# Reordering the first batch of a retention and wave-MLP kernel around its fourth pair

## The chip, the cores and the metric

The kernel runs on one core of a Trainium2 chip. The metric is the time of one execution on the device in microseconds (us). TensorE is called PE here, its weight loads PEld, VectorE DVE, ScalarE ACT, GpSimd POOL and SyncE SP, as in the profile.

## What is computed

There are B = 4 batches, H = 8 heads, S = 768 steps and head size D = 64. First comes a retention recurrence, then a token and channel mixer on its output x of shape (4, 768, 512):

```
state = gamma[h] * state + outer(k[t], v[t])
x[t]  = scale * (q[t] @ state)                  # per batch and head

theta = x @ w_theta
zr, zi = x * cos(theta), x * sin(theta)
y = w_tok_r @ zr + w_tok_i @ zi                 # over the tokens of a batch
u = x + y
out = u + max(u @ w_ch, 0)
```

All inputs and the output are float32. The kernel multiplies in bfloat16.

## The kernel before

**Pairs.** The 768 steps of a batch are cut into three pairs of 2 x 128 steps, so that there are twelve pairs n = 0 to 11, of which 0, 1 and 2 are the first batch. Even and odd steps of a pair are kept apart ("two" in the code). For each pair, `load` brings q, k and v (512 KB each) with one DMA each into a ring of seven buffers. `prep` (L162) casts k to bfloat16 (one instruction on ACT, L169, or elsewhere, L171) and multiplies q and v with the powers of gamma (two halves each, L175, each on a chosen engine: `DP` is DVE and POOL, `PP` twice POOL). `flip` (L179) turns k or q with eight PE transposes into PSUM and copies them out on DVE (L186); later pairs use a DMA transpose instead (`flip_dma`, from pair 7 for k, pair 10 for q).

**Retention.** `ret_A` multiplies turned k and q, `ret_mask` (L211, DVE) applies the causal mask, `ret_Y` adds mask times v, `ret_I` (L241) adds the part of the state, `ret_S` (L258) adds to the state in PSUM, `state_out` (L272, ACT) copies it out, and `ret_out` (L281) copies a half of the result to `xT`. 

**Mixer.** `theta` multiplies xT with w_theta, and ACT makes cosine and sine of it (`cs`, L305 and L306). `x_pe` turns xT back to x (L295, copy L296 on DVE); later pairs do that by DMA. `zmul` (L312, DVE) makes z. `moe_M` (L328) multiplies one row tile of the token weights with all six z tiles of a batch, step s0 by step s0, two matmuls each. `moe_u` (L335, DVE) adds x, `moe_U` turns u (copy L349 on ACT), `moe_O` (L356) multiplies with w_ch, `moe_out` (L363, DVE) finishes, `store` writes a tile. The token weights come as rows: `w_cast` casts a row tile of both parts on POOL (L375) into a ring of three row buffers, `w_tok` turns it with twelve PE transposes (L382) and copies it out, one part on DVE, one on ACT (L386, L388).

**PSUM.** A ring of two buffers, tag "tr", serves all transposes and also `moe_O`. A ring of two, "acc", serves theta and the two halves of `ret_Y`. One bank "at" serves `ret_A`, one bank "st" the state, one bank "y" the sum of `moe_M` until late in the kernel. An instruction that writes a buffer waits until the last reader of its former content is done.

**Order.** There is no scheduler. Each engine runs its instructions in the order in which the Python code issues them. For the first three pairs this order is written out by hand (L450 to L555), and the loop over n at L565 issues the rest: in round n it does the retention of pair n, the theta and z of pair n - 1, the mixer's tiles of the batch before, and the preparation of later pairs. `keep_busy` (L445) issues matmuls on zeros whose result is not used. SP's queue of loads is written out at L111 for the first six pairs and the weights: p0, w_theta, p1, w0, p2, w1, w2, p3, w3, w_ch, p4, w4, p5, w5. Round n issues the loads of pair n + 3.

The round n = 3 (nG is 3) in before prepares pair 4 early: `prep` of q and v on POOL as its first step, `flip` of k and q in its middle, ahead of `ret_S(3, 0)`.

Of the kernel before, what the change touches and what calls it, by code (L numbers as in the profile page):

```python
# [14 lines left out]
FT = mybir.dt.float32  # L15
# [17 lines left out]
def kernel(  # L33
# [142 lines left out]
                                        _bcast_last(sc[:, 2 * g + two], D))  # L176
        st[n, name] = t

    def flip(n, name):  # L179
        ps = psum.tile([P, 2, NP, P], BF, name="kq_ps", tag="tr", bufs=2)  # L180
        for two in range(2):
            for j in range(NP):
                nc.tensor.transpose(ps[:, two, j, :],  # L183
                                    st[n, name][:, two, j * P:(j + 1) * P], ident)
        t = work.tile([P, 2, NP, P], BF, name="kqT", bufs=6)
        nc.vector.tensor_copy(t, ps)  # L186
        st[n, name + "T"] = t

    def flip_dma(n, name):
        t = work.tile([P, 2, NP, P], BF, name="kqT", bufs=6)  # L190
# [18 lines left out]
    def ret_mask(n, two):  # L209
        at, at_ps = work.tile([P, 2, NP, P], BF, name="at", bufs=2), st[n, "at_ps"]  # L210
        nc.vector.tensor_mul(at.rearrange("p a j t -> p (a j) t"),  # L211
                             at_ps.rearrange("p a j t -> p (a j) t"),
                             _bcast_mid(maskp[:, two].rearrange("p w i -> p (w i)"), H))
        st[n, two] = at
# [72 lines left out]
            out=xs[b][:, 2 * g:2 * g + 2, :].rearrange("p a (j e) -> p (a j) e", j=NP),  # L287
            in_=st[n, "xT"].rearrange("p a j t -> p (a j t)"))

    def x_pe(n, lo=0, hi=2):  # L290
        b, g = divmod(n, nG)
        x_ps = psum.tile([P, hi - lo, NP, P], BF, name="x_ps", tag="tr", bufs=2)
        for a in range(lo, hi):
            for j in range(NP):
                nc.tensor.transpose(x_ps[:, a - lo, j, :], st[n, "xT"][:, a, j, :], ident)  # L295
        nc.vector.tensor_copy(xs[b][:, 2 * g + lo:2 * g + hi, :],  # L296
                              x_ps.rearrange("p a j e -> p a (j e)"))

    def theta(n, a):
        th_ps = psum.tile([P, dm], FT, name="th_ps", tag="acc", bufs=2)  # L300
# [16 lines left out]
    def moe_M(m, lo, hi):  # L317
        b, t0 = divmod(m, nT)
        if lo == 0:
            if m < (B - 1) * nT - 1:  # L320
                y_ps = psum.tile([P, dm], FT, name="y_ps", tag="y", bufs=1)
            else:
                y_ps = psum.tile([P, dm], FT, name="y_ps", tag="acc", bufs=2)
            mo[m] = dict(y=y_ps)
        y_ps = mo[m]["y"]
        for s0 in range(lo, hi):
            for r in range(2):
                nc.tensor.matmul(y_ps, wT[r][:, s0, t0 * P:(t0 + 1) * P],  # L328
                                 zs[b][:, s0, r, :], start=(s0 == 0 and r == 0),
                                 stop=(s0 == nT - 1 and r == 1))  # L330
# [40 lines left out]

    def w_cast(t0):
        for r in range(2):
            row = work.tile([P, S], BF, name="wrow", bufs=3)
            nc.gpsimd.tensor_copy(row, wdma[r, t0])  # L375
            wrow[r, t0] = row

    def w_tok(t0):
        for r in range(2):
            w_ps = psum.tile([P, nT, P], BF, name="w_ps", tag="tr", bufs=2)  # L380
            for s0 in range(nT):
                nc.tensor.transpose(w_ps[:, s0, :],  # L382
                                    wrow[r, t0][:, s0 * P:(s0 + 1) * P], ident)
            dst = wT[r][:, :, t0 * P:(t0 + 1) * P]
            if r:
                nc.scalar.copy(dst, w_ps)  # L386
            else:
                nc.vector.tensor_copy(dst, w_ps)  # L388

    def moe_last(m):  # L390

# [53 lines left out]
    def keep_busy(times):  # L445
        for _ in range(times):
            nc.tensor.matmul(warm_ps, warm[:, 0:P], warm, start=True, stop=True)


    DP, PP, K = (nc.vector, nc.gpsimd), (nc.gpsimd, nc.gpsimd), (nc.scalar,)  # L450
    keep_busy(12)
    prep(0, "k", K)
    flip(0, "k")
    keep_busy(4)
    prep(0, "q", DP)
    flip(0, "q")
    keep_busy(2)
    prep(0, "v", PP)
# [3 lines left out]
    keep_busy(2)  # L462
    ret_S(0, 0)
    state_out(0, 0)
    keep_busy(1)
    ret_A(0, 1)
    ret_mask(0, 1)
    ret_S(0, 1)
    state_out(0, 1)
    ret_Y(0, 0)  # L470
    ret_I(0, 1)
    keep_busy(3)
    prep(1, "k", K)
    ret_Y(0, 1)
    ret_out(0, 0, nc.scalar.copy)
    ret_out(0, 1, nc.vector.tensor_copy)
    keep_busy(1)
    flip(1, "k")
    prep(1, "q", DP)
    x_pe(0, 0, 1)  # L480
    theta(0, 0)
    x_pe(0, 1, 2)
    theta(0, 1)
    flip(1, "q")
    keep_busy(2)
    prep(1, "v", PP)
    w_cast(0)
    ret_A(1, 0)
    ret_mask(1, 0)
    keep_busy(2)  # L490
    ret_S(1, 0)
    state_out(1, 0)
    ret_A(1, 1)
    ret_mask(1, 1)
    prep(2, "k", K)
    ret_Y(1, 0)
    ret_I(1, 0)
    ret_S(1, 1)
    state_out(1, 1)
    ret_I(1, 1)  # L500
    keep_busy(2)
    zmul(0, 0)
    zmul(0, 1)
    ret_Y(1, 1)
    ret_out(1, 0, nc.scalar.copy)
    w_tok(0)
    ret_out(1, 1, nc.scalar.copy)
    prep(2, "q", DP)
    flip(2, "k")
    theta(1, 0)  # L510
    flip(2, "q")
    prep(2, "v", PP)
    w_cast(1)
    w_cast(2)
    x_pe(1, 0, 1)
    moe_M(0, 0, 2)
    ret_A(2, 0)
    ret_mask(2, 0)
    theta(1, 1)
    x_pe(1, 1, 2)  # L520
    ret_S(2, 0)
    state_out(2, 0)
    ret_A(2, 1)
    ret_mask(2, 1)
    ret_Y(2, 0)
    ret_I(2, 0)
    ret_I(2, 1)
    zmul(1, 0)
    zmul(1, 1)
    ret_Y(2, 1)  # L530
    ret_out(2, 0, nc.scalar.copy)
    ret_out(2, 1, nc.vector.tensor_copy)
    w_tok(1)
    theta(2, 0)
    x_pe(2, 0, 1)
    theta(2, 1)
    x_pe(2, 1, 2)
    moe_M(0, 2, 4)
    zmul(2, 0)
    prep(3, "k", K)  # L540
    w_tok(2)
    moe_M(0, 4, 5)
    zmul(2, 1)
    flip(3, "k")
    moe_M(0, 5, nT)
    moe_u(0)
    prep(3, "q", DP)
    prep(3, "v", PP)
    w_cast(3)
    moe_M(1, 0, 4)  # L550
    flip(3, "q")
    moe_M(1, 4, nT)
    moe_u(1)
    w_tok(3)
    prep(4, "k", K)  # L555


    tiles_of = {nG - 2: [], nG - 1: [0, 1]}
# [6 lines left out]
    for n in range(nG, B * nG + 1):  # L565
        mine, done = tiles_of[n], tiles_of[n - 1]
        late, two = n > nG, len(mine) > 1
        nxt = n + 1 in pairs

        if nxt and n + 1 >= K_DMA:  # L570
            flip_dma(n + 1, "k")
        if n + 3 in pairs:
            load(n + 3, "k")
        if n >= U_DMA:
            moe_U_dma(done[1])

        if nxt:
            prep(n + 1, "q", PP)
            prep(n + 1, "v", PP)
        if n == nG:  # L580
            w_cast(4)
            nc.gpsimd.tensor_copy(wch, wdma["ch"])
        if n == nG + 1:
            w_cast(5)
        if late:
            ret_I(n - 1, 1)

        if n in pairs:
            ret_A(n, 0)
            ret_mask(n, 0)  # L590
        if late:
            ret_Y(n - 1, 1)
            ret_S(n - 1, 1)
            ret_out(n - 1, 0, nc.scalar.copy)
            ret_out(n - 1, 1, nc.scalar.copy)
            state_out(n - 1, 1)
            if n - 1 >= X_DMA:
                x_dma(n - 1)
        if n + 3 in pairs:
            load(n + 3, "q")  # L600

        first = mine[0]
        moe_M(first, 0, 3 if two else 2)
        if late:
            theta(n - 1, 0)
            if n - 1 < X_DMA:
                x_pe(n - 1)
            theta(n - 1, 1)
        if two:
            moe_M(first, 3, nT)  # L610
            moe_u(first)
        for name, limit in (("k", K_DMA), ("q", Q_DMA)):
            if nxt and n + 1 < limit:
                flip(n + 1, name)
        if not two and n + 1 >= K_DMA:
            moe_M(first, 2, 4)
        if nxt and n + 1 >= Q_DMA:
            flip_dma(n + 1, "q")
        if n + 3 in pairs:
            load(n + 3, "v")  # L620
        for t in tiles_of[n - 2]:
            store(t)
        if n + 1 >= U_DMA:
            moe_U_dma(first)

        if n in pairs:
            ret_S(n, 0)
            state_out(n, 0)
            ret_A(n, 1)
            ret_mask(n, 1)  # L630
            ret_Y(n, 0)
            ret_I(n, 0)
        if n < U_DMA:
            moe_U(done)
        if not two:
            if n + 1 < K_DMA:
                moe_M(first, 2, 4)
            if n in (nG, nG + 1):
                w_tok(n - nG + 4)
            moe_M(first, 4, nT)  # L640
            moe_u(first)
        elif n in pairs:
            moe_M(mine[1], 0, nT)
        if n + 2 in pairs:
            prep(n + 2, "k", K)
        if late:
            zmul(n - 1, 0)
            zmul(n - 1, 1)
        if two and n in pairs:
            moe_u(mine[1])  # L650
        for t in done:
            moe_O(t)
            moe_out(t)
        if n not in pairs:
            moe_M(mine[1], 0, nT)
            moe_u(mine[1])
# [43 lines left out]
```

## Time and profile before

| what | us |
|---|---|
| median of 11 runs | 172.37 |
| lowest and highest | 171.77 to 174.01 |
| the profiled execution | 172.63 |
| span in its profile | 170.9 |
| busy: PE, PEld | 158.5, 89.8 |
| busy: DVE, ACT, POOL | 100.8, 82.6, 62.7 |
| HBM read, written | 25.69 MB, 6.29 MB |

The profile is of one execution. Times in its views run from the start of the span. A busy PE is not yet a PE at its peak, since the matmuls are pipelined: 128 x 512 matmuls are listed with 380 ns each and follow each other every 216 ns. A wait is put down to the instruction that released it last.

### The profile page before, as it was taken

How to read it: one execution, taken by the hardware profiler on the slowest of the kernel's cores; microseconds unless marked ns; L12 is line 12 of the kernel's file. 1: busy time of each engine (PE TensorE's matmuls, PEld its weight loads, DVE VectorE, ACT ScalarE, POOL GpSimd, SP SyncE). 2: the span in 40 equal slices, each digit the busy share in tenths (PEclk: the TensorE clock that was granted, in tenths of full speed). 3: DMA queues.
4: the chain of work that ended last, by engine and by line, in shares of the span. 5: the costliest groups of instructions: out<-in, count | busy, mean ns of one | idle time of the engine just before them, and what ended most of it. 6: DMA issues, size and time to landing. Idle time of an engine off the chain costs nothing.

```text
span 170.9 us, 4674 instructions
## 1 busy us (share of the span) xinstructions
PE 158.5 (93%) x1952; PEld 89.8 (53%) x1979; DVE 100.8 (59%) x139; ACT 82.6 (48%) x141; POOL 62.7 (37%) x81
## 2 busy tenths in 40 slices
PE   7789898979599999999999999999999999999992
PEld 2355565645375766655465655554455544444471
DVE  2357597885457567798477375681755617333443
ACT  8216686770345968767874744828156170000000
POOL 6274839383599678480807254000000000000000
PEclk9999999999969999999999999999999999999999
DMA  4999999999999999989999995986827251554343
GB/s 123 303 342 313 319 316 348 266 377 308 325 287 306 297 294 341 260 192 233 197 282 308 214 278 110 256 101 129 151 44 200 36 168 47 163 157 117 92 153 123
DMA packets 66789, 37.92 MB, mean 222 GB/s; under 512 B 24144, under 2 KB 61264, under 8 KB 66768
## 3 DMA queue, kind: packets, MB, share of 16 engines
q1 hardware_dynamic: 66624, 37.50, 86.8%
q8 instruction: 15, 0.25, 0.6%
q10 hardware_dynamic: 144, 0.13, 0.2%
q14 instruction: 6, 0.05, 0.1%
HBM read 25.69 MB, written 6.29 MB: 187 GB/s over the span
## 4 chain that ended last, share of the span: by engine, by line
PE 79%; DMA 9%; DVE 3%; ACT 3%; issue 2%; POOL 1%; DVEq 0%; POOLq 0%
PE y_ps L328 32%; PE o_ps L356 12%; PE th_ps L302 12%; DMA pair<-in_q_dram 6%; PE at_ps L204 4%; PE kq_ps L183 4%; PE yT_ps L227 4%; PE st_ps L258 3%; PE yT_ps L241 3%; DMA pair<-in_k_dram 2%; PE y_ps L402 2%; PE w_ps L382 2%; DVE at L211 1%; PE u_ps L347 1%; ACT kqb L169 1%
## 5 line engine op out<-in xcount | busy, mean ns | idle before, releaser
L328 PE MATMUL y_ps<-z,wtr 128*128 128x512 bf16 x132 | 50.1, 380 | 1.6 <-DVE u L335 0.9
L328 PE MATMUL y_ps<-z,wti 128*128 128x512 bf16 x123 | 46.7, 380 | 0.5 <-issue 0.2
L175 POOL TENSOR_TENSOR kqb<-pair,qscp 128x512 bf16<-128x512 f32 x20 | 20.6, 1046 | 35.2 <-DMA pair<-in_q_dram 35.2
L335 DVE TENSOR_TENSOR u<-y_ps,x_sb 128x512 bf16<-128x512 f32 x23 | 15.9, 691 | 29.2 <-PE y_ps L328 29.2
L211 DVE TENSOR_TENSOR at<-at_ps,maskp 128x1024 bf16<-128x1024 f32 x24 | 29.2, 1218 | 3.8 <-PE at_ps L204 3.8
L281 ACT CAST xT<-yT_ps 128x512 bf16<-128x512 f32 x22 | 15.0, 738 | 25.7 <-PE yT_ps L227 25.7
L175 POOL TENSOR_TENSOR kqb<-pair,vscp 128x512 bf16<-128x512 f32 x24 | 26.2, 1114 | 2.2 <-DMA pair<-in_v_dram 2.2
L302 PE MATMUL th_ps<-wth,xT 128*128 128x512 bf16 x94 | 23.4, 379 | 0.2
L363 DVE SCALAR_TENSOR_TENSOR ot<-o_ps,u 128x512 f32<-128x512 f32 x23 | 15.8, 689 | 12.4 <-PE o_ps L356 12.4
L356 PE MATMUL o_ps<-wch,uT 128*128 128x512 bf16 x92 | 22.7, 379 | 0.1
L272 ACT CAST stbd<-st_ps 64x256 bf16<-64x256 f32 x40 | 14.7, 368 | 13.2 <-PE st_ps L258 12.5
L328 PEld LDWEIGHTS <-wti 128*128 128x128 bf16 x138 | 13.6, 98 | 14.2 <-issue 1.4
L328 PEld LDWEIGHTS <-wtr 128*128 128x128 bf16 x138 | 13.6, 98 | 14.0 <-issue 0.3
L305 ACT ACTIVATE cs<-th_ps,halfpi 128x512 bf16<-128x512 f32 x24 | 16.5, 689 | 8.3 <-PE th_ps L302 8.0
L186 DVE COPY kqT<-kq_ps 128x1024 bf16<-128x1024 bf16 x17 | 11.5, 687 | 12.4 <-PE kq_ps L183 12.4
L312 DVE TENSOR_TENSOR z<-cs,x_sb 128x1024 bf16<-128x1024 bf16 x24 | 17.1, 748 | 0.7 <-DMA x_sb<-xT 0.7
L306 ACT ACTIVATE cs<-th_ps,zerob 128x512 bf16<-128x512 f32 x24 | 16.5, 688 | 0.0
L356 PEld LDWEIGHTS <-uT 128*128 128x128 bf16 x92 | 8.8, 98 | 10.7 <-ACT uT L349 0.4
L302 PEld LDWEIGHTS <-xT 128*128 128x128 bf16 x96 | 8.9, 98 | 9.9 <-ACT xT L281 0.6
L183 PE MATMUL kq_ps<-ident,kqb 128*128 128x128 bf16 x136 | 10.5, 222 | 3.4 <-POOL kqb L175 1.2
L169 ACT CAST kqb<-pair 128x1024 bf16<-128x1024 f32 x12 | 12.6, 1048 | 1.7 <-DMA pair<-in_k_dram 1.6
L414 ACT COPY uT<-u_ps 128x256 bf16<-128x256 bf16 x2 | 0.7, 372 | 25.6 <-PE u_ps L413 25.6
(57 smaller groups left out, 163.7 us busy)
## 6 DMA issues: line engine op xcount, KB each, us to landing
pair<-in_k_dram SPq DMA_DIRECT2D x12, 512.0 KB, 6.8
pair<-in_q_dram SPq DMA_DIRECT2D x12, 512.0 KB, 7.4
pair<-in_v_dram SPq DMA_DIRECT2D x12, 512.0 KB, 7.7
out_dram<-ot SPq DMA_DIRECT2D x23, 256.0 KB, 2.4
wtok<-in_moe_w_tok_r_dram SPq DMA_DIRECT2D x6, 384.0 KB, 6.9
wtok<-in_moe_w_tok_i_dram SPq DMA_DIRECT2D x6, 384.0 KB, 6.0
w<-in_moe_w_theta_dram SPq DMA_DIRECT2D x1, 1024.0 KB, 8.0
w<-in_moe_w_ch_dram SPq DMA_DIRECT2D x1, 1024.0 KB, 7.2
```

The lines of the kernel that those rows point to most:

```text
L175: engines[two].tensor_mul(dst[:, two], src[:, two], _bcast_last(sc[:, 2 * g + two], D))
L183: nc.tensor.transpose(ps[:, two, j, :], st[n, name][:, two, j * P:(j + 1) * P], ident)
L211: nc.vector.tensor_mul(at.rearrange("p a j t -> p (a j) t"), at_ps.rearrange("p a j t -> p (a j) t"), _bcast_mid(maskp[:, two].rearrange(" ...
L281: copy(st[n, "xT"][:, a].rearrange("e j (i w) -> e j w i", w=2), st[n, "y"][a].rearrange("e j (w i) -> e j w i", w=2))
L302: nc.tensor.matmul(th_ps, st[n, "xT"][:, a, j, :], wth[:, j, :], start=(j == 0), stop=(j == NP - 1))
L305: nc.scalar.activation(cs[:, 0, :], th_ps, AF.Sin, bias=halfpi, scale=1.0)
L306: nc.scalar.activation(cs[:, 1, :], th_ps, AF.Sin, bias=zerob, scale=1.0)
L312: nc.vector.tensor_mul(zs[b][:, c], st[n, "cs", a], _bcast_mid(xs[b][:, c, :], 2))
L328: nc.tensor.matmul(y_ps, wT[r][:, s0, t0 * P:(t0 + 1) * P], zs[b][:, s0, r, :], start=(s0 == 0 and r == 0), stop=(s0 == nT - 1 and r == 1))
L335: nc.vector.tensor_add(u, mo[m]["y"], xs[b][:, t0, :])
L356: nc.tensor.matmul(o_ps, mo[m]["uT"][:, j, :], wch[:, j, :], start=(j == 0), stop=(j == nD - 1))
L363: nc.vector.scalar_tensor_tensor(ot, mo[m]["o"], 0.0, mo[m]["u"], ALU.max, ALU.add)
```

## The change

Nothing is computed differently, and the instructions on PE are the same but for four `keep_busy` matmuls fewer (27 for 31). What changes is order, engine and buffer.

- Pair 0: q is scaled ahead of the copy of k's transposes on DVE (`flip` without a copy, then `flip_out`). Both halves of `ret_out(0)` run on DVE.
- Pairs 0 to 2: x is turned with one group of eight transposes and one copy instead of two groups of four; the copy of x(0) stands behind the first mask of pair 1, the copy of x(1) is on ACT. Theta stands ahead of the flips or between them. `ret_out(1)` is split over ACT and DVE.
- The cast of k of pairs 2, 3 and 5 is on POOL, of pair 4 on ACT in round 3.
- The rows of w are turned in single parts (`w_flip`, `w_out`): row tile 0 inside pair 1's retention, row tile 2's first part copied on ACT, its second part in round 3. Row tile 3 goes into round 3, 4 into round 4, 5 into round 5: one round later than before for 4 and 5.
- `wrow` has five buffers instead of three.
- The sum of `moe_M` for tile 1 is in the bank "st", which is idle between the first and the second batch, so tiles 0 and 1 are open at the same time. Their last steps stand in round 3, behind `ret_A(3, 0)`.
- Round 3: w_ch is cast first on POOL. Pair 4's k (ACT), q (DVE and POOL) and v are prepared behind `moe_U`, and its two flips stand at the end of the round, one ahead of each `moe_O`.

The core of the diff (the split of `w_tok` into `w_flip` and `w_out`, and of `x_pe` into `x_pe` and `x_out`, is left out):

```diff
@@ flip
-    def flip(n, name):
+    def flip(n, name, copy=nc.vector.tensor_copy):
...
-        nc.vector.tensor_copy(t, ps)
-        st[n, name + "T"] = t
+        if copy:
+            copy(t, ps)
+        st[n, name + "T"], st[n, name + "_ps"] = t, ps
+
+    def flip_out(n, name):
+        nc.vector.tensor_copy(st[n, name + "T"], st[n, name + "_ps"])
@@ moe_M
-            if m < (B - 1) * nT - 1:
+            if m == 1:
+                y_ps = psum.tile([P, dm], FT, name="y_ps", tag="st", bufs=1)
+            elif m < (B - 1) * nT - 1:
@@ w_cast
-            row = work.tile([P, S], BF, name="wrow", bufs=3)
+            row = work.tile([P, S], BF, name="wrow", bufs=5)
@@ the order of pairs 0 to 2: pair 2 on
-    prep(2, "k", K)
...
-    w_tok(0)
-    ret_out(1, 1, nc.scalar.copy)
+    ret_out(1, 1, DV.tensor_copy)
+    w_flip(1, 0)
+    prep(2, "k", (PL,))
+    zmul(0, 0)
+    flip(2, "k")
     prep(2, "q", DP)
-    flip(2, "k")
     theta(1, 0)
+    zmul(0, 1)
+    theta(1, 1)
+    moe_M(0, 0, 1)
     flip(2, "q")
     prep(2, "v", PP)
     w_cast(1)
     w_cast(2)
-    x_pe(1, 0, 1)
-    moe_M(0, 0, 2)
+    x_pe(1, AC.copy)
+    moe_M(0, 1, 2)
...
     w_tok(1)
+    moe_M(0, 2, 3)
+    prep(3, "k", (PL,))
+    moe_M(0, 3, 4)
     theta(2, 0)
-    x_pe(2, 0, 1)
+    flip(3, "k")
+    prep(3, "q", DP)
     theta(2, 1)
-    x_pe(2, 1, 2)
-    moe_M(0, 2, 4)
+    x_pe(2)
+    w_flip(0, 2, False)
+    w_out(0, 2, AC.copy)
+    moe_M(1, 0, 2)
     zmul(2, 0)
-    prep(3, "k", K)
-    w_tok(2)
-    moe_M(0, 4, 5)
-    zmul(2, 1)
-    flip(3, "k")
-    moe_M(0, 5, nT)
-    moe_u(0)
-    prep(3, "q", DP)
+    flip(3, "q")
     prep(3, "v", PP)
     w_cast(3)
-    moe_M(1, 0, 4)
-    flip(3, "q")
-    moe_M(1, 4, nT)
-    moe_u(1)
-    w_tok(3)
-    prep(4, "k", K)
+    moe_M(1, 2, 4)
+    zmul(2, 1)
+    moe_M(0, 4, 5)
@@ the loop
-        if nxt:
-            prep(n + 1, "q", PP)
+        def preps(engines):
+            prep(n + 1, "q", engines)
             prep(n + 1, "v", PP)
+            if n in (nG, nG + 1):
+                w_cast(n - nG + 4)
+
         if n == nG:
-            w_cast(4)
             nc.gpsimd.tensor_copy(wch, wdma["ch"])
         if n == nG + 1:
-            w_cast(5)
+            prep(n + 1, "k", (PL,))
+        if nxt and n > nG:
+            preps(PP)
...
+        if n == nG:
+            moe_M(0, 5, nT)
+            w_flip(1, 2)
+            moe_u(0)
+            moe_M(1, 4, nT)
+            moe_u(1)
...
-            if nxt and n + 1 < limit:
+            if nxt and nG + 1 < n + 1 < limit:
                 flip(n + 1, name)
...
+        if n == nG:
+            prep(n + 1, "k", (AC,))
+            preps(DP)
+        if n == nG or n + 1 < K_DMA and not two:
+            moe_M(first, 2, 4)
+        if n < nG + 3:
+            w_tok(n - nG + 3)
...
-        if n + 2 in pairs:
-            prep(n + 2, "k", K)
+        if n + 2 in pairs and n > nG:
+            prep(n + 2, "k", (AC,))
...
-        for t in done:
+        for i, t in enumerate(done):
+            if n == nG:
+                flip(n + 1, "kq"[i])
             moe_O(t)
             moe_out(t)
```

## The prediction

> **What bounds the kernel now.** I read the page's slices first, then TensorE's waits, the chain of waits, the timelines of PE and POOL around the place they name, and last a table of windows. The slices of the page:
>
> ```profile
> PE   7789898979599999999999999999999999999992
> ...
> PEclk9999999999969999999999999999999999999999
> DMA  4999999999999999989999995986827251554343
> ```
>
> One slice is 170.9/40 = 4.27 us. From slice 12 on (51 us) PE is full to the end: what follows is PE work, and only its start can move. Before that, PE has holes, and slice 11 (47.0 to 51.3) has the one drop of the granted clock. The DMA engines are full through slice 17 (77 us), so the arrival of a pair of q, k, v is a date that hardly moves. The waits of PE and the chain of waits:
>
> ```profile
> PE kq_ps L183 <- POOL kqb L175: 1.2, 2, 0.6
> ...
> PE y_ps L328 <- DVE u L335: 0.9, 1, 0.9
> ...
> PE kq_ps L183 <- ACT kqb L169: 0.7, 2, 0.5
> ```
>
> ```profile
> 33.53 10.80 DMA pair<-in_q_dram
> 44.46 2.05 POOL kqb L175 x2
> ```
>
> So pair 4's q (issued 33.53, landed 44.46), scaled on POOL until 46.5, is what the flips of pair 4 wait for, and the chain runs through it. PE there (start, length, instructions, and in brackets the wait):
>
> ```profile
> 44.33 0.62 PE L183 MATMUL kq_ps<-ident,kqb 128*128 128x128 bf16 x8 [0.52 <-ACT kqb L169]
> 45.56 0.40 PE L183 MATMUL kq_ps<-ident,kqb 128*128 128x128 bf16 x4 [0.61 <-POOL kqb L175]
> 46.56 0.61 PE L183 MATMUL kq_ps<-ident,kqb 128*128 128x128 bf16 x4 [0.60 <-POOL kqb L175]
> 47.10 0.53 PE L258 MATMUL st_ps<-kqb 64*64 64x64 bf16 x12
> ```
>
> Between 43.9 and 47.1 PE has sixteen transposes and nothing else. The windows around it (busy time of each engine, the clock, the DMA share, GB/s):
>
> ```profile
> 33.00:43.70 10.70, 9.53 (x92) 5.49 (x91) 7.18 (x12) 5.23 (x8) 5.91 (x5) 1.00 1.08 325
> 43.70:47.10 3.40, 1.67 (x18) 1.02 (x17) 1.14 (x2) 0.57 (x1) 2.64 (x3) 0.92 1.00 339
> 47.10:50.10 3.00, 2.78 (x59) 2.40 (x60) 1.92 (x2) 1.24 (x3) 3.00 (x5) 0.53 1.07 289
> ```
>
> PE idles 1.17 us in the first, 1.73 in the second, and runs the third at 0.53 of its clock, which loses 3.0 x 0.47 = 1.41. That is 4.3 us to be had behind 33 us.
>
> [...] VectorE's half of a q (L175) took 0.72 to 1.27 us here, longest beside POOL work. I take 1.0.
>
> **The landmark.** Round n = 4 of the loop begins on PE with the state's product of pair 3 (L241), at 53.77 before. From there PE is full in both kernels, if the data is there, so the change is worth what this date moves, less work pushed past it. Prices on PE, from the chain: eight transposes 0.45; theta 0.86; one s0 of M (two matmuls) 0.43; a row tile of w, both parts, 0.67; ret_A 0.35; ret_Y 0.35; ret_S 0.27; O 0.86. VectorE: mask 1.22, copy of eight transposes 0.69, z 0.65, u 0.69, xT 0.73, wtr 0.56; ScalarE: each cs 0.6 in a row, xT 0.73, wti 0.80, k 1.05. A hand-over between engines costs 0.05 to 0.2.
>
> *Removed filler.* 31 keep_busy become 27: 4 x 0.216 = 0.9 us of PE, but they stood in front of waits, so nothing by itself; the price, if PE falls to half clock, is the 1.4 us above. My walk leaves no gap over 0.6 us, so I take nothing.
>
> *Pairs 0 and 1, reordered.* q0's scaling goes before the copy of k0's flip on VectorE: it starts at the landing (7.03) instead of 7.46, and ret_A(0,0) goes from 10.08 to about 9.7. Both xT on VectorE (13.85 to 15.2) bring theta(0,0) forward, and x's transposes leave the way of pair 1's flips: ret_A(1,0) from 18.94 to 18.1. Splitting ret_out(1) over ScalarE and VectorE ends the row that put xT(1,1) at 25.04: 23.0 now. Then pair 2's q, landed at 23.77, binds in both: half on VectorE to 25.1, z, flip, copy, and ret_A(2,0) at 26.95 instead of 27.19. All of this is worth 0.24 at that point.
>
> *Pair 2.* k2 (landed 21.92) and k3 (about 31.8, before q3's 33.54) go from ScalarE to POOL. L169's 1.05 becomes, by L459's 1.89 us for 2048 columns, about 1.0 there; what is queued behind, q2 and q3, lands later than POOL is done. If k3 landed 1 us later, q3's half would be 1 us later. x(1)'s copy goes from VectorE to ScalarE, 1.01 us by uT's copy of this shape (L349), and ends at 27.8, before z(1,0) needs it at 30.3. ScalarE gets free: cs no longer holds the bank for ret_Y (the 0.48 us wait at 29.93). Five row buffers instead of three end POOL's 1.85 us wait at 31.88; POOL has slack, so nothing. The masks of pair 2 stay a chain: 28.6, 30.37; ret_Y(2,1) at 30.4 instead of 30.90; z(1,1) at 32.25 releases M's fourth step.
>
> *Tile 1 in the state's bank, pair 3.* In before, k3's cast stood behind four cs on ScalarE and q3's half behind u(0) on VectorE: flips at 36.63 and 40.35, ret_A(3,0) at 42.42. Now flip k3 runs at 33.6, q3's half 34.85 to 35.85, the copy of x to 36.45, the flip of q3 at 36.6, its copy to 37.9. M of tile 1 has the idle state bank, so its first four steps fill PE from 35.75 to 37.95 without waiting for u(0) (the 0.94 us wait). ret_A(3,0) at 38.45, its mask to 40.17, u(0) to 40.8, u(1) to 41.4. Tile 2 waits for u(0), 0.4 us; ret_S(3,0) waits for u(1), which is over when M's first two steps end at 41.7. ret_A(3,1), ret_Y, U: PE at 43.1. Before had U at 48.5.
>
> *Round n = 3 from there.* M 0.86, w tile 3 0.67, M 0.86: PE at 45.5. VectorE is through the mask at 43.7 and then stands at q4, which lands at 44.46; with 1.0 for the half it is free at 45.5, copies wtr to 46.05, and only this frees the transposes' buffer for flip k4 (both "tr" buffers are taken). PE idles 0.6 there: this is the new wait. ScalarE meanwhile: uT to 44.2, k4 to 45.25, wti to 46.05, no later. Flip k4 46.1, O(0) 46.55 to 47.4, flip q4 47.45, then O(1) waits for the buffer until 48.25 and runs 48.3 to 49.15. Round 4 begins at 49.15: 4.6 earlier.
>
> *Pushed past it.* w tile 4 moves to round 4, tile 5 to round 5: 0.67 of PE returns. wch's cast is off POOL by 41.8, and O(0) is due at 46.5. No DMA moves: SyncE's queue holds the same transfers in the same order, and of its waits only some change the engine that frees a buffer, long before the issue.
>
> *Is the data there?* POOL: q4's half 45.5, v4 to 48.25, w4 to 50.0, k5 (moved from ScalarE) to 51.1, q5 (no later than 51.84 by the trace; from 2.36 MB at some 310 GB/s before q6's 58.96, about 51.3) to 53.4. Flip q5 is due 4.6 behind the round's start, 53.8: 0.4 in hand. If k5 stays on POOL until 52, 0.3 is lost. q6 (58.96, ready 61.0) is due at 63.4; q7 (64.91, ready 67.0) at 72.2; SyncE's queue, never idle before 69 us, reaches the DMA transpose of k7 at 69.1, landed by 75.2, due at 76.7. So the gain stays.
>
> **The sum.** 4.6 - 0.67 = 3.9 us. The profiled execution took 172.63 (span 170.9, 1.7 around it): 168.7. The median of the runs is 0.26 lower, 172.37: 168.5.
>
> **Rivals.** (a) More hand-overs than walked: some twenty of these lie between 27 and 49 us, and 0.1 more in each is 2.0, gain 1.9: 170.5. For it: VectorE ran 7.18 of 10.7 us already and gets two halves more. (b) Pair 5 binds: POOL takes k5, w4 and q5 in one row. If both land 0.7 us later than they did (k5 then at 52.0, casts to 53.05, q5's two halves to 55.1), flip q5 slips from 53.8 to 55.2: 1.4 lost, 169.9. Against it: q5 was found landed at 51.84, and the loads stand in SyncE's queue as before. (c) The stall comes back whole: later pairs bind at their landing, 172.3; against it, the 2 us in hand at q6. (d) Slower: VectorE's half of q4 holds wtr, u(2) and both flips. Each microsecond that q4 lands later stalls PE as long[...]. From a landing at 47 the gain is 3.9 - 2.5 - 1.4 = 0; at 49, 4.5 + 1.4 - 3.9 = 2.0 lost, 174.4. Against it: q4's buffer is free ten microseconds ahead and its 10.9 us from issue to landing is already the longest of the loads. That the move isn't made can't be: the order of the built program shows pair 4's q behind pair 3's masks.
>
> **Chances.** The forecast (167.7 to 169.3) 0.60; (a) 0.16; (b) 0.15; (c) 0.04; (d) 0.05. The low end is the limit that q5 sets (flip q5 from 58.4 to 53.4 less 0.67 is 4.3, so 168.0) with 0.3 for an earlier landing, the high end takes in (a) and (b): 167.7 to 170.6. About 0.3% (0.5 us) can be told from no change; only (c) is inside, only (d) beyond: 0.91, 0.04, 0.05.
>
> **What would show it.** Right: round 4's L245 matmuls at about 49.2, no slice of low clock, ret_A(3,0) near 38.5, a PE wait of about 0.6 on wtr before flip k4, and PE full from there. Wrong: a POOL wait on k5 or q5 that PE's flips of pair 5 inherit (b); a VectorE wait on q4 much behind 44.5 (d); masks and copies of pair 3 later than walked (a).

## The result, and the profile after

The changed kernel takes 169.97 us (median of 12 runs, 169.28 to 172.04), the kernel before beside it 172.33 (47 runs, 171.33 to 174.89). The ratio is 0.9866, 95% interval [0.9842, 0.9890]: 2.36 us faster, where 3.9 were forecast. Ratios here leave out runs in which the chip was disturbed, so they are not always the quotient of the medians shown. The profiled execution took 170.26 with a span of 168.6, against 172.63 and 170.9.

The slices of the page after (busy tenths of PE, its granted clock, the DMA engines):

```profile
PE   7669887598999999999999999999999999999990
...
PEclk9999999999999999999999999999999999999999
DMA  4999999999999999999999998949644161753443
```

Counted from 0, the drop in slice 11 is gone, and PE is full from slice 10 on. But slice 7 (29.5 to 33.7) now has a 5. The waits of PE say what it is (total, times, longest):

```profile
PE y_ps L340 <- DVE z L322: 1.7, 2, 1.4
PE at_ps L208 <- DVE at L215: 1.4, 3, 0.7
```

M waits 1.4 us for one z, which it did not do before. The chain of waits through that place (start, length, what):

```profile
29.34 1.22 DVE at L215
30.57 1.20 DVE z L322
31.76 0.65 DVE xT L285
32.41 1.15 DVE z L322
33.55 0.04 issue
33.59 0.59 PE y_ps L340 x2
```

The chain through pair 4's q of before is gone; in its place VectorE's row of a mask, two z and a copy leads to PE. From the timeline of PE, that wait, pair 4's two flips, and the landmark, round 4's first L245:

```profile
33.59 0.38 PE L340 MATMUL y_ps<-z,wtr 128*128 128x512 bf16 x1 [1.40 <-DVE z L322]
46.80 0.61 PE L183 MATMUL kq_ps<-ident,kqb 128*128 128x128 bf16 x8
48.34 0.61 PE L183 MATMUL kq_ps<-ident,kqb 128*128 128x128 bf16 x8
49.93 0.39 PE L245 MATMUL yT_ps<-kqT,stbd 128*128 128x128 bf16 x4
```

The flips start without a wait, and the landmark stands at 49.93: 3.84 earlier than 53.77, where 4.6 were forecast. The windows, which answer to those of before:

```profile
27.00:33.00 6.00, 3.74 (x102) 2.85 (x103) 4.93 (x6) 3.21 (x6) 4.97 (x6) 1.00 1.10 322
33.00:43.70 10.70, 9.68 (x127) 5.72 (x129) 7.96 (x11) 4.12 (x7) 7.68 (x8) 1.00 1.08 328
43.70:49.93 6.23, 6.00 (x69) 3.75 (x59) 5.02 (x7) 3.29 (x5) 5.08 (x6) 1.00 1.12 323
```

The last row is the stage that the change aims at: PE idles 0.23 us in it at full clock, where before it idled 1.73 in 43.70 to 47.10 and then ran at 0.53. The first row holds what went wrong: PE idles 2.26 us in six, where before it idled 0.59:

```profile
27.00:33.00 6.00, 5.41 (x113) 3.46 (x113) 5.30 (x8) 3.42 (x6) 3.54 (x5) 1.00 1.12 301
```

Only a part of this is the z: in k3_act below, where both z are short, PE still idles 1.88 us there, and the landmark comes 1.04 earlier.

The dates that matter, of every kernel measured here, from each one's trace ("PE's end" is the end of its last matmul, "tail" the span less that) and from its times. The first four columns are of one execution each, and a span is given to 0.1 us. The medians come from different chips, so kernels are compared by their ratios, each to the kernel before beside it:

| kernel | landmark | PE's end | tail | span | median us | ratio to before, 95% interval |
|---|---|---|---|---|---|---|
| before | 53.77 | 167.71 | 3.19 | 170.9 | 172.33 | |
| changed | 49.93 | 164.74 | 3.86 | 168.6 | 169.97 | 0.9866 [0.9842, 0.9890] |
| slots_alone | 50.92 | 165.50 | 3.20 | 168.7 | 170.30 | 0.9872 [0.9843, 0.9901] |
| no_slots | 53.58 | 168.29 | 3.81 | 172.1 | 172.62 | 0.9999 [0.9970, 1.0027] |
| k3_act | 48.89 | 165.90 | 4.00 | 169.9 | 170.87 | 0.9897 [0.9852, 0.9943] |
| rows3 | 49.11 | 164.60 | 4.00 | 168.6 | 170.52 | 0.9874 [0.9830, 0.9919] |
| act_pad | 50.17 | 165.66 | 3.24 | 168.9 | 170.61 | 0.9857 [0.9818, 0.9896] |
| xfirst | 49.75 | 164.67 | 3.73 | 168.4 | 170.73 | 0.9883 [0.9847, 0.9919] |
| k3_xfirst | 48.98 | 164.22 | 3.68 | 167.9 | 169.78 | 0.9838 [0.9807, 0.9870] |
| best | 50.15 | 165.14 | 3.26 | 168.4 | 170.13 | 0.9863 [0.9824, 0.9902] |
| xfirst_warm | 49.11 | 163.68 | 3.72 | 167.4 | 169.71 | 0.9839 [0.9797, 0.9881] |
| best_warm | 49.10 | 164.17 | 3.23 | 167.4 | 169.34 | 0.9818 [0.9775, 0.9861] |

PE ends 2.97 us earlier in the changed kernel, but the span shrinks by 2.3: the tail behind PE grew by 0.67.

### The profile page after: what moved, and what is told of

It reads as the page before. It is cut to its first block, busy times and chain, and to the rows that moved or that the text cites. A ratio compares the mean times of both kernels' runs of the same rounds, so it can differ in the third digit from the quotient of the medians.

```text
span 168.6 us, 4659 instructions
## 1 busy us (share of the span) xinstructions
PE 154.9 (92%) x1949; PEld 88.4 (52%) x1975; DVE 102.4 (61%) x137; ACT 80.2 (48%) x138; POOL 65.5 (39%) x83
## 4 chain that ended last, share of the span: by engine, by line
PE 75%; DVE 8%; SPq 7%; DMA 5%; issue 2%; POOL 1%; DVEq 0%
PE y_ps L340 34%; PE o_ps L368 12%; PE th_ps L312 10%; DMA pair<-in_k_dram 5%; SPq L81 5%; DVE z L322 4%; PE kq_ps L183 3%; PE at_ps L208 3%; PE yT_ps L231 3%; PE st_ps L262 3%; PE yT_ps L245 2%; DVE at L215 2%; PE w_ps L393 2%; PE y_ps L419 2%; SPq L95 1%
## 5 line engine op out<-in xcount | busy, mean ns | idle before, releaser
L340 PE MATMUL y_ps<-z,wti 128*128 128x512 bf16 x122 | 46.2, 379 | 0.4 <-issue 0.2
L285 ACT CAST xT<-yT_ps 128x512 bf16<-128x512 f32 x20 | 13.5, 737 | 27.9 <-PE yT_ps L231 27.9
L322 DVE TENSOR_TENSOR z<-cs,x_sb 128x1024 bf16<-128x1024 bf16 x24 | 18.7, 808 | 1.5 <-DMA x_sb<-xT 1.4
L187 DVE COPY kqT<-kq_ps 128x1024 bf16<-128x1024 bf16 x16 | 10.9, 687 | 5.2 <-PE kq_ps L183 5.2
L208 PE MATMUL at_ps<-kqT 64*64 64x128 bf16 x384 | 10.6, 221 | 2.2 <-DVE at L215 1.4
```

The lines of the kernel that those rows point to most:

```text
L208: nc.tensor.matmul(at_ps[half, par, j, :], kT[rows, two, j, half], qT[rows, :, j, half], start=(j == 0), stop=(j == NP - 1), skip_group_ch ...
L322: nc.vector.tensor_mul(zs[b][:, c], st[n, "cs", a], _bcast_mid(xs[b][:, c, :], 2))
L340: nc.tensor.matmul(y_ps, wT[r][:, s0, t0 * P:(t0 + 1) * P], zs[b][:, s0, r, :], start=(s0 == 0 and r == 0), stop=(s0 == nT - 1 and r == 1))
```

## The experiments

My theory after the result: the move of pair 4's preparation and flips makes the gain; the 0.76 us missing at the landmark is the z that ran beside GpSimd; the rest is lost behind PE. The rivals: the new order of the first batch makes the gain, and the missing part is many small hand-overs (rival a of the prediction).

**Which part makes the gain.** slots_alone is the kernel before with only round 3's move:

```diff
-    prep(4, "k", K)
...
+        if n == nG:
+            prep(n + 1, "k", K)
+            prep(n + 1, "q", DP)
+            prep(n + 1, "v", PP)
+            w_cast(4)
...
-            if n in (nG, nG + 1):
-                w_tok(n - nG + 4)
+            if n in (nG + 1, nG + 2):
+                w_tok(n - nG + 3)
...
+            if n == nG:
+                flip(n + 1, "kq"[i])
             moe_O(t)
```

> The kernel before, with one part of the change: pair 4's preparation and flips in round 3 behind moe_U and ahead of each moe_O, w tiles 4 and 5 one round later; the first batch's order, three row buffers and tile 1's bank as before. If the slots carry the gain (theory: what PE won is the wait for q4 and the half clock behind it), round 4 begins on PE at about 50.0 (before 53.77, after 49.93), no slice has a low clock, and the time is 169.5 to 170.3. If the new order of the first batch carries it (rival), the slots alone give under 1 us: 171.4 or more, because q4 lands at 43.6 to 44.5 whatever PE does.

no_slots is the changed kernel with that move undone: k cast ahead of the loop, q and v on POOL at the start of the round (behind the cast of w_ch), both flips ahead of `ret_S(3, 0)`. The tiles of w stay where the changed kernel has them.

> The kernel after, with that one part undone: pair 4's k is cast ahead of the loop, its q and v are scaled on POOL as round 3's first step, and its flips stand ahead of ret_S(3, 0) again. Theory of the slots: flip of q4 at about 46, 5.5 us of PE work behind it and the clock perhaps halved again, so round 4 begins at 51.8 to 53.3 and the time is 171.8 to 173.2. Rival (order of the first batch): round 4 begins by 50.7, 170.7 or less.

slots_alone gives 170.30, no_slots 172.62, both as the theory had it, though their landmarks came later than expected (50.92 for about 50.0, 53.58 for 51.8 to 53.3). So the move alone has all of the gain that the times can show (0.9872 against 0.9866), and the new order with the move undone has none (0.9999). By the traces the order is not idle: on top of the move it brings the landmark from 50.92 to 49.93 and PE's end from 165.50 to 164.74, 0.76 us, and the longer tail (3.86 for 3.20) takes 0.66 of that. Why the order is worth nothing in no_slots shows in its timelines of ScalarE and PE:

```profile
43.02 1.04 ACT L169 CAST kqb<-pair 128x1024 bf16<-128x1024 f32 x1 [5.64 <-DMA pair<-in_k_dram]
43.97 0.79 ACT L400 COPY wti<-w_ps 128x768 bf16<-128x768 bf16 x1
```

```profile
44.81 0.39 PE L340 MATMUL y_ps<-z,wti 128*128 128x512 bf16 x1 [2.99 <-ACT wti L400]
```

Being early, ScalarE stands 5.64 us in front of pair 4's k, which is there only at 43.02 (in before ScalarE took it at 43.23 without a wait); the copy of wti is queued behind that cast, PE waits 2.99 us for it, and then runs at 0.62 of its clock for 3 us (the window 44.8 to 47.8). Here work that comes early runs into a landing, unless something is put in front of the wait; the move does just that. My undoing is harsher than the kernel before, since there the copy of wti stood ahead of k's cast: what the new order would give alone with that copy ahead was not measured.

**The z beside GpSimd.** From the timelines of VectorE and POOL, changed kernel:

```profile
30.48 1.28 DVE L322 TENSOR_TENSOR z<-cs,x_sb 128x1024 bf16<-128x1024 bf16 x1
32.31 1.24 DVE L322 TENSOR_TENSOR z<-cs,x_sb 128x1024 bf16<-128x1024 bf16 x1
```

```profile
30.40 0.83 POOL L387 CAST wrow<-wtok 128x768 bf16<-128x768 f32 x1 [0.29 <-DMA wtok<-in_moe_w_tok_i_dram]
31.96 1.04 POOL L171 CAST kqb<-pair 128x1024 bf16<-128x1024 f32 x1 [0.74 <-DMA pair<-in_k_dram]
```

And before, the same two:

```profile
30.59 1.28 DVE L312 TENSOR_TENSOR z<-cs,x_sb 128x1024 bf16<-128x1024 bf16 x2
```

```profile
31.88 0.83 POOL L375 CAST wrow<-wtok 128x768 bf16<-128x768 f32 x1 [1.85 <-PE w_ps L382]
```

Before, two z took 1.28 together, while POOL stood in its 1.85 us wait (30.03 to 31.88). Now each takes as much alone: the second starts at 32.31 beside the cast of k3, which ends at 33.00, and ends 0.55 after that; the first ends 0.53 after the cast of w beside it (31.23). The theory of the next runs, which they call exclusion: a z and the POOL instruction beside it lengthen each other. Two ways to take POOL's work away from z:

```diff
-    prep(3, "k", (PL,))
+    prep(3, "k", (AC,))
```

> The kernel after, with k of pair 3 cast on ScalarE instead of POOL. Exclusion theory [...]: z(1,1), 1.24 us beside that cast in after, takes 0.65 to 0.7, PE's wait of 1.40 us for it falls to about 0.8, and the time falls by 0.2 to 0.6: 169.4 to 169.8. Rival (many hand-overs a little longer than reckoned): z stays at 1.2, no change within 0.2.

```diff
-            row = work.tile([P, S], BF, name="wrow", bufs=5)
+            row = work.tile([P, S], BF, name="wrow", bufs=3)
```

> The kernel after, with three row buffers instead of five. Exclusion theory: POOL's cast of w2's second part waits for PE's w transposes again (to 31.3), so z(1,0), 1.28 us in after, takes 0.65 and xT(2,1) follows 0.6 earlier; z(1,1) then meets that cast or k3's and still takes 1.0 to 1.3, so PE's wait shrinks by 0 to 0.7: 169.3 to 170.0. Rival (the buffers gave POOL time that counts): q3's half comes later and the time rises by 0.3 or more, 170.3 up.

The two z of k3_act:

```profile
30.42 0.68 DVE L322 TENSOR_TENSOR z<-cs,x_sb 128x1024 bf16<-128x1024 bf16 x1
31.69 0.67 DVE L322 TENSOR_TENSOR z<-cs,x_sb 128x1024 bf16<-128x1024 bf16 x1
```

For z the expectation held: both are short and the landmark comes to 48.89. The cast of w that begins 0.04 behind the first of them (30.46) takes 1.33 instead of 0.83: there it is POOL that loses. In rows3 one of the two z (0.68) is free of POOL and the landmark comes to 49.11. The time did not follow: both medians lie above the expected range, at ratios of 0.9897 and 0.9874. That of rows3 (170.52) is what its rival expected, but not for the rival's reason: VectorE begins q3's half at 35.41, 0.73 earlier than in the changed kernel.

A trace taken for another purpose shows how much of this is chance. pool_casts, below, is the changed kernel, instruction for instruction, until past 100 us. In its execution POOL's casts fell elsewhere against the same two z:

```profile
30.45 0.98 DVE L322 TENSOR_TENSOR z<-cs,x_sb 128x1024 bf16<-128x1024 bf16 x1
31.99 0.92 DVE L322 TENSOR_TENSOR z<-cs,x_sb 128x1024 bf16<-128x1024 bf16 x1
```

Each ends 0.54 us after the cast beside it, as the two in the changed kernel's own trace do (0.53 and 0.55), but the casts began earlier (k3's at 31.33 instead of 31.96), and the landmark stands at 49.22. Ordered by the sum of the two z, the landmarks are: 1.35 (k3_act) 48.89, 1.67 (k3_xfirst) 48.98, 1.90 (pool_casts) 49.22, 1.91 (rows3) 49.11, 2.52 (xfirst) 49.75, 2.52 (changed) 49.93. So the landmark follows the two z, and what POOL adds to them differs between executions of one kernel.

PE of k3_act stops later, and VectorE's timeline shows for what:

```profile
90.51 0.81 PE L340 MATMUL y_ps<-z,wtr 128*128 128x512 bf16 x2 [2.20 <-DVE u L347]
```

```profile
88.56 1.29 DVE L322 TENSOR_TENSOR z<-cs,x_sb 128x1024 bf16<-128x1024 bf16 x2 [3.78 <-DMA x_sb<-xT]
```

The microsecond gained at 49 is given back, and more, at 90, where z stands behind x, which comes by a DMA transpose. Three rows of SP's queue:

```profile
79.64 3.13 SPq L195 DMA_TRANSPOSE kqT<-kqb  x1
82.86 0.53 SPq L81 DMA_DIRECT2D pair<-in_k_dram  x1
83.49 2.00 SPq L290 DMA_TRANSPOSE x_sb<-xT  x1
```

x is turned behind k's transpose (3.13) and behind the load of k. The six times of k3_act fall into two groups, 169.51 to 170.22 and 171.53 to 171.66; the profiled execution (171.63) is of the second. That this stall makes the difference between the groups is likely, but no execution of the first was profiled.

pool_casts stops at the same place, 14 us before its extra work on POOL begins:

```profile
89.41 0.81 PE L340 MATMUL y_ps<-z,wtr 128*128 128x512 bf16 x2 [0.97 <-DVE u L347]
```

The changed kernel's own trace, with the later landmark, has no such wait, and nothing is left at PE's end of what pool_casts had gained at the landmark (164.81 against 164.74). rows3 waits 0.86 there. So in these three traces most or all of what faster z give at 49 us is taken back at 90.

**The exclusion by itself.** Late in the kernel POOL is idle, so there it can be loaded with work whose results are not used:

```diff
+        if n == B * nG - 1:
...
+            for _ in range(36):
+                nc.gpsimd.tensor_copy(scr_o, scr_i)
```

> The kernel after, and POOL, idle from 102 us on, runs 36 casts of 128x1024 float32 to bfloat16 on a scratch tile that nobody reads. In after the eight z from 107 us on take 0.68 us each, u 0.69, the mask 1.22. Exclusion theory: [...] the z between 102 and 140 take 0.7 to 1.75, mean about 1.2, casts next to a z reach 1.6, and u, mask and the other instructions with an input in PSUM keep their times within 0.02. Rival (the long z come from ScalarE or the DMAs): z stays at 0.68.

pool_muls has multiplications of 128x512 instead:

> The kernel after, and POOL runs 36 float32 multiplications of 128x512 in that place, the form of L175, on a scratch tile that nobody reads. Exclusion theory: as with the casts, z of 0.7 to 1.75 up to 140 us, with u and mask unchanged. If only POOL's casts do it, z stays at 0.68 here.

The groups between 107 and 139 us (number, then busy time and mean ns of one), first with casts:

```profile
L607 POOL CAST scr_o<-scr_i 128x1024 bf16<-128x1024 f32 x28 | 31.5, 1126 | 1.8
L322 DVE TENSOR_TENSOR z<-cs,x_sb 128x1024 bf16<-128x1024 bf16 x7 | 8.0, 1177 | 0.0
L215 DVE TENSOR_TENSOR at<-at_ps,maskp 128x1024 bf16<-128x1024 f32 x5 | 6.1, 1219 | 0.0
L347 DVE TENSOR_TENSOR u<-y_ps,x_sb 128x512 bf16<-128x512 f32 x6 | 4.1, 684 | 11.5 <-PE y_ps L340 11.5
```

with multiplications:

```profile
L607 POOL TENSOR_TENSOR scr_o<-scr_i 128x512 bf16<-128x512 f32 x23 | 31.2, 1356 | 1.8
L322 DVE TENSOR_TENSOR z<-cs,x_sb 128x1024 bf16<-128x1024 bf16 x7 | 10.4, 1512 | 0.0
```

and in the changed kernel, where POOL does nothing there:

```profile
L322 DVE TENSOR_TENSOR z<-cs,x_sb 128x1024 bf16<-128x1024 bf16 x8 | 5.1, 682 | 0.0
L347 DVE TENSOR_TENSOR u<-y_ps,x_sb 128x512 bf16<-128x512 f32 x6 | 4.1, 691 | 13.5 <-PE y_ps L340 13.5
```

z, with both inputs in SBUF, grows from 0.68 to 1.18 and 1.51 on average; u and the mask, with one input in PSUM, keep their length (0.68 and 1.22 beside the casts, 0.69 and 1.22 without). POOL's casts take 1.13 on average, where those of k3 and k5 in the changed kernel took 1.04. The prediction took 1.0 for q's half, from 0.72 to 1.27 us that it found in before, and made no such allowance for z.

**The order of SP's queue.** Rounds 6 to 8 with the load of k(n + 3) behind the transposes of x, and k3 on ScalarE:

```diff
-        if n + 3 in pairs:
+        if n + 3 in pairs and n - 1 < X_DMA:
             load(n + 3, "k")
...
                 x_dma(n - 1)
+                if n + 3 in pairs:
+                    load(n + 3, "k")
```

> The kernel of run k3_act, with the load of k of pair n + 3 behind the DMA transpose of x in rounds 6 to 8 instead of ahead of it. Supply theory (the transpose of x in round 7, held in SyncE's queue behind loads, makes z, u and the bank of M late, so that PE waits 2.2 us in k3_act): that wait falls below 0.5, PE is done 1.0 us before after's, and the time is 168.9 to 169.3. Rival (the transposes are slow whatever stands ahead, or the k load now comes late): the wait stays above 1.5, or moves to pair 9 to 11's k, and the time stays at 170.5 or more.

The wait near 90 shrinks from 2.20 to 0.61:

```profile
88.82 0.81 PE L340 MATMUL y_ps<-z,wtr 128*128 128x512 bf16 x2 [0.61 <-DVE u L347]
```

0.9838 is the best ratio so far. But wait and median (169.78) are above what the theory expected, PE is done only 0.52 earlier than in the changed kernel, and the interval overlaps with those of k3_act and of the changed kernel. The queue alone, with k3 left on POOL:

> The changed kernel with only the load of k(n + 3) moved behind the transposes of x in rounds 6 to 8 (k3 stays on GpSimd). If the transposes of x bind only once PE is earlier (theory): nothing to gain here, since round 8 begins 1 us later than with k3 on ScalarE and z(6) is not late: 0.984 to 0.988 of the kernel before, the changed kernel's own 0.987 within the interval. If the queue already bound in the changed kernel (rival): as good as the variant with both edits, 0.984 or less, with round 8 starting where it did and a later round earlier by 0.5 or more.

0.9883, within the changed kernel's own interval, and its landmark and PE's end hardly move. This fits the theory that the transposes of x bind once PE comes earlier. They do not bind by the landmark alone: act_pad, with 50.17, waits 0.58 there, the changed kernel, with 49.93, does not.

**The tail.** The last output DMA that ScalarE issues, in the timelines of before, of after, and of act_pad:

```profile
168.31 0.37 ACTq L439 DMA_DIRECT2D out_dram<-oh  x1
```

```profile
165.35 1.00 ACTq L456 DMA_DIRECT2D out_dram<-oh  x1
```

```profile
166.26 0.37 ACTq L459 DMA_DIRECT2D out_dram<-oh  x1
```

In the changed kernel the DMA view of 163 to 169 us has a packet that before has not:

```profile
q14 instruction: 1, 0.01, 0.6%
```

act_pad adds three one-element copies on ScalarE at the start, whose results are not used:

```diff
+    for i in range(3):
+        sp = const.tile([P, 1], FT, name=f"pad{i}")
+        nc.scalar.copy(sp, zerob)
```

> The kernel after, with three copies of 128x1 on ScalarE, whose results are not used, ahead of the first k. In after ScalarE's last DMA issue takes 1.00 us with an instruction transfer in that window; before has 0.37 and three ScalarE instructions more. Theory of the instruction stream: the transfer falls elsewhere, the last issue takes 0.37, from PE's last matmul to the end of the span it is 3.2 us instead of 3.9, and the time falls by 0.5 to 0.7, to about 169.4. Rival (the longer end comes from PE's earlier end or chance): it stays at 1.0 and 3.9, and the time within 0.2.

The issue is back at 0.37, the packet of instructions is gone from the end, and the tail is 3.24. Over all fourteen traces the split is clean: 0.37, a tail of 3.19 to 3.26 and no packet of instructions behind 163 us with 141 or more busy instructions on ScalarE; 0.87 to 1.19, 3.68 to 4.00 and one such packet with 138 or 139. The profile does not say which engine a packet is for; that it is ScalarE's is inferred from this split. How three copies move the packet was not shown. The median did not show it (170.61 for about 169.4): act_pad's trace has PE at half clock from 31 to 34 (more on that below) and PE's end 0.92 later.

**All together, and the clock.**

> The changed kernel with k3's cast back on ScalarE, the load of k(n + 3) behind the transposes of x in rounds 6 to 8, and three one-element ScalarE copies at the start whose results are not used. If the three findings add up: round 4's first L245 near 49.0 (49.93 in the changed kernel), no PE wait above 0.7 behind 88 us, the last output DMA issued by ScalarE in 0.37 us instead of 1.00, PE's last matmul about 1 us before the changed kernel's 164.7, and a ratio near 0.980 to the kernel before. If the time at the end only moves to another transfer, or the pads shift nothing that counts: no better than 0.984, the ratio of the variant with the first two edits.

0.9863: no better. The three findings did not add up. In the profiled execution the windows of best show why (columns as above, the clock third from the end):

```profile
24.00:27.00 3.00, 2.95 (x27) 1.78 (x26) 2.53 (x4) 2.25 (x4) 2.34 (x3) 1.00 0.89 292
27.00:31.00 4.00, 2.56 (x90) 1.92 (x88) 2.93 (x4) 1.81 (x4) 3.92 (x5) 1.00 1.05 319
31.00:34.00 3.00, 2.78 (x29) 1.87 (x20) 2.38 (x4) 2.08 (x3) 0.15 (x1) 0.50 1.21 294
```

After four microseconds with PE busy for 2.56, mostly with small products, PE is granted half its clock for three. The same stretch (2.55 or 2.56 busy) stands in ten traces: in those of best, act_pad and pool_muls the half clock follows, in those of no_slots, k3_act, rows3, k3_xfirst, xfirst and pool_casts, and of the changed kernel, it does not. pool_muls is the changed kernel instruction for instruction until past 100 us, so this differs from execution to execution. In before and slots_alone, whose traces show no drop there, PE is busy for 3.52 in that stretch.

The timed runs say how often this happens, since the mean granted clock of each is on record. The traces with a drop of this size have a mean of 0.985 to 0.990, those without 0.994 to 1.000, and no timed run lies between. Of the 50 runs of the nine kernels with the thin stretch (no_slots left out, which has its own drop at 44.8), 14 are at 0.990 or below; of the 18 of slots_alone and of the two kernels with fillers below, none. The mean does not tell where in a run the drop falls. Nor does the drop explain best's median: its runs with the lower mean took 170.08, 170.09 and 171.42, those at 1.000 took 169.72, 170.18 and 170.21. Why the three edits do not add up in the timed runs stays open.

The last two kernels fill the stretch, with matmuls on zeros whose results are not used (this is best_warm; xfirst_warm is without the ScalarE pads):

```diff
     state_out(2, 0)
+    fill = psum.tile([P, dm], FT, name="fill", tag="tr", bufs=2)
+    for _ in range(3):
+        nc.tensor.matmul(fill, warm[:, 0:P], warm, start=True, stop=True)
     ret_A(2, 1)
...
     ret_I(2, 1)
+    for _ in range(2):
+        nc.tensor.matmul(fill, warm[:, 0:P], warm, start=True, stop=True)
     ret_Y(2, 1)
```

> The variant with all three edits, whose trace shows PE at 0.50 of its clock from 31 to 34 us, plus five 128x512 matmuls on zeros whose results are not used: three ahead of ret_A(2, 1), which waits 0.72 there, and two ahead of ret_Y(2, 1), which waits 0.55. If the thin work on PE between 27 and 31 us draws the half clock (theory): clock 1.00 in every window from 24 to 51, M's fourth step no later than 32.7, round 4's first L245 at 49.0 instead of 50.15, and 1.0 to 1.2 us saved: about 0.980 of the kernel before. If the half clock comes from the shifted start and not from the thin stretch (rival): it stays at 31 to 34, or shows at another place, and the ratio stays at 0.984 to 0.988.

> The same without the three ScalarE pads: k3's cast on ScalarE, the load of k(n + 3) behind the transposes of x, and the five filler matmuls whose results are not used. Its trace without the fillers had the full clock, so if the clock does not vary from run to run the fillers buy nothing: 0.984 of the kernel before, landmark 49.0, last ScalarE DMA issue 0.9. Against the padded kernel beside it: if the pads' shorter last issue counts, 0.3 to 0.6 us slower than it; if it does not, equal within the interval. If the half clock also hits some timed runs of the kernel without fillers: faster than 0.984 by up to 0.003.

The same windows of best_warm:

```profile
27.00:31.00 4.00, 3.61 (x95) 2.25 (x93) 2.88 (x4) 1.75 (x4) 4.00 (x5) 1.00 1.12 327
31.00:34.00 3.00, 2.53 (x32) 1.45 (x23) 2.26 (x4) 2.48 (x3) 0.65 (x2) 1.00 1.19 306
```

The clock holds, the landmark is at 49.10 and PE ends 0.97 before best. (The trace of xfirst_warm holds its clock too, but so did that of k3_xfirst, without the fillers.) best_warm, at 0.9818, has the lowest ratio of all; against 0.9866 that is some 0.8 us, though the two intervals overlap. Its margin over xfirst_warm (0.0021) is within them too, and the spans of the two are equal: the pads' 0.49 in the tail is set off by 0.49 that PE ends later. What the pads are worth in the end is open.

## Why the prediction was right, and where it was off

The mechanism and the sign were right: the wait for q4 and the half clock behind it are gone, and the move made that gain. The forecast 168.5 was 1.5 us too low, and the result lies in the range.

- *Pairs 0 to 2.* ret_A(0,0) was forecast at 9.7, ret_A(1,0) at 18.1, ret_A(2,0) at 26.95 and ret_Y(2,1) at 30.4; measured 9.67, 18.11, 27.13 and 30.62. Right to 0.2.
- *"z(1,1) at 32.25 releases M's fourth step".* It did so at 33.55: 1.3 late. This step failed, by two terms: "z 0.65", a price from a time when POOL was idle, and "Five row buffers ... POOL has slack, so nothing". POOL's wait was the cover under which z ran at 0.68; the buffers and k3's move filled it. k3_act puts z's end back at 32.36 and the landmark at 48.89, 0.26 before the forecast 49.15, so this one term explains the landmark. Its size in one trace is partly luck: pool_casts has the landmark at 49.22.
- *From there the walk held, late.* Flip k3 was forecast at 33.6, flip q3 at 36.6, ret_A(3,0) at 38.45, flip k4 at 46.1, flip q4 at 47.45; measured 34.89, 37.84, 39.68, 46.80, 48.34. The forecast 0.6 us wait in front of flip k4 did not occur, since PE came later: it took up half of the 1.3, and 0.78 was left at the landmark. (In k3_act, where flip k4 comes at 45.77, a gap of some 0.2 stands there.)
- *No low clock, q5 in time.* Right in the changed kernel's trace: behind 50 us the only listed wait of PE is of 0.16. The price of 1.4 was somewhat high: best's landmark is 1.17 behind k3_xfirst's, that of pool_muls 0.95 behind that of pool_casts. But "my walk leaves no gap over 0.6 us, so I take nothing" was an estimate that did not hold (the changed kernel has waits of 0.72 and 1.40), and it was no reason either. Single gaps don't decide: best lost the clock behind gaps of 0.72 and 0.55 with small products between them, and in before, whose clock fell to 0.53 behind the window 43.70 to 47.10, PE was busy for 1.67 of its 3.40 us. In no_slots 0.62 for 3 us followed a PE wait of 2.99.
- *A price read from one execution.* Of the 51 timed runs of before that stand beside the experiments, 16 have a mean clock of 0.979 to 0.990, as the profiled one has (0.990), and 35 have 0.996 or more; their medians are 173.11 and 172.25. So a drop like the one that the prediction prices at 1.41 of 4.3 us was probably there in a third of the executions only, and the forecast took it from a median in which it is mostly absent. How much of the 1.5 this makes is not measured.
- *"0.67 of PE returns".* Round 5 took 9.09 before and 10.00 now: 0.91. The 0.24 beyond is again z beside POOL: two z at 59.64 took 2.61 beside q6's halves, and the copy of x and the flip behind them slid. The other kernels with the same work in round 5 bear this out: where those two z took 1.28 to 2.13 together, the round took 9.76 or 9.77, which is the forecast 0.67; with 2.50 to 2.81 it took 9.90 to 10.21.
- *"Is the data there?"* The prediction followed pair 5's q, q6, q7 and k7, and left out the DMA transposes of x. The changed kernel's trace has no wait for them, but k3_act (2.20), pool_casts (0.97) and rows3 (0.86) have: had z kept its price, this would have taken back much of what that gave.
- *The end.* The sum let everything behind PE stand. It grew by 0.67, with the number of instructions on ScalarE; I had not looked at what stands behind PE's last matmul.

By the two profiled executions alone: forecast 3.9; less 0.76 at the landmark, less 0.24 in round 5, less 0.67 in the tail gives 2.2, and the span shrank by 2.3.

Rival (b) came nearest in time (169.9), then (a) (170.5), both by the wrong way: the casts of q5 were done at 53.3, pair 5's flips began at 54.12 and waited for nothing, and what was lost against the walk sits in a few z and in the tail, not in many hand-overs. Rivals (c) and (d) did not occur either: q4 landed by 43.7. Their kind was seen elsewhere, however: no_slots is (c), at a landing, and k3_act is a later supply that binds, at x instead of q5.

What stays open: why the same thin stretch costs the clock in some executions only. A busier PE there kept it in two of two traces and twelve of twelve runs, where three of ten traces had lost it and 14 of 50 runs have the lower mean; that is support, not proof. Seven of the 14 are among the 12 runs of the two kernels with the pads, so the pads may have a part in it, by a way that nothing here shows.

## What to carry to other kernels

A wait may be the cover for something else. Before taking one away, list what the freed engine will run then, and what runs beside it. In this kernel z, a VectorE operation with both inputs in SBUF, took 1.18 or 1.51 us on average beside GpSimd for 0.68 alone. Early work is worth what the next fixed date leaves of it: find the next landing or transpose in the queue before counting a gain, and look at what stands behind PE's last matmul, where every microsecond counts in full. A profile is one execution: before you price a stall or a low clock from it, see in how many of the timed runs it can be there.

## What the runs showed of the hardware

- Where a cast of GpSimd had begun first, VectorE's z ended 0.53 to 0.55 us after the cast's end, in the traces of the changed kernel, rows3 and pool_casts; with GpSimd idle it takes 0.68. Where z had begun first (k3_act), it took 0.68 and the cast 1.33 for 0.83.
- Beside GpSimd's casts VectorE's z went from 0.68 to 1.18 us on average, beside its multiplications to 1.51; operations with one input in PSUM kept 0.68 and 1.22. GpSimd loses too: its casts took 1.13 on average there for 1.04.
- The last DMA issue on ScalarE took 0.37 us, or 0.87 to 1.19 when a packet of instructions fell into the end. With three tiny copies at the start (act_pad) it was 0.37, without them (the changed kernel) 1.00.
- PE went to 0.50 of its clock for 3 us after four microseconds in which it was busy for 2.56, in three traces of ten with the same stretch, and in neither of the two with five more 128x512 matmuls. Of 50 runs with the stretch 14 have a mean clock low enough for such a drop (0.990 or less), of the 12 with the five matmuls none.
